# Experts of 448 places with shared half tiles, and row halves for the last channels, in a fused RWKV-7 and hash-routed mixture kernel

## The chip, the cores and the metric

One core of one Trainium2 chip runs the whole kernel. The metric is the device time of one execution in microseconds, as the median of several runs. All arithmetic is in float32.

## The reference

The reference has two stages. The first is a recurrent attention over 768 steps for 4 batches and 8 heads of 40 channels; per head it keeps a 40 x 40 state. Its result is laid out as 3,072 token rows of 320 channels. The second stage sends each row through one of 8 experts, picked by a hash of the token's id.

```python
for t in range(S):                       # S = 768
    y[:, :, t] = einsum('bhd,bhde->bhe', rt, state)
    Sa = einsum('bhde,bhe->bhd', state, at)
    state = state * wt[:, :, None, :] - einsum('bhd,bhe->bhde', Sa, bt) + einsum('bhd,bhe->bhde', vt, kt)
x = y.transpose(0, 2, 1, 3).reshape(3072, 320)
expert_idx = token_ids * 2654435761 % 8
for e in range(8):                       # w1[e]: 320 x 1024, w2[e]: 1024 x 320
    out[mask_e] = maximum(x[mask_e] @ w1[e], 0) @ w2[e]
```

The token ids are drawn with a fixed seed; by them the experts get 387, 359, 415, 376, 364, 403, 371 and 397 tokens.

## The kernel before

**Attention.** The 768 steps are cut into chunks of 64, and two batches make one tile, so there are 24 tiles (`NU`). Each tile passes through a chain of small matrix products (lines 361 to 664), most of them on 40 or 64 rows and 40 or 64 columns of TensorE, with the heads spread over upper and lower row halves and left and right column halves. The order of all this is written out by hand: each piece of work is put into a plan with a tick (`at_tick`, line 249), roughly one tick per tile, and the plan is run sorted by tick (line 800). Engines other than SyncE's queue (SP) keep exactly this order. SP issues the loads of r, v, a, b, k and w (line 240 and others), in program order, each waiting for its buffer. POOL issues the loads of decay products, the stores of finished rows to the DRAM tensor `x_rows` (line 652), and all indirect transfers.

**Routing.** `routing()` (line 688) is a generator whose pieces are put between the attention work from tick 8 on, half a tick apart (line 794). It counts the tokens per expert with two matrix products, gives each token a place in a list of 512 places per expert (`SLOTS`), writes the 3,072 token numbers into the DRAM list `slot_tokens` by 24 indirect writes (line 767), and reads the list back with one transfer (line 774) as `idx_all`, 128 places per column. Empty places hold the number 3,072, and `src_all` is the same list with those cut to the last row.

**Experts.** When attention is done (line 802), the memory of its pools goes to the experts' tiles. Four tiles of 128 places make one expert (`TPE`), and all 512 places are computed. For each expert (line 861):

- `gather` (line 821) brings 128 rows of `x_rows` by an indirect transfer on POOL, turns them with three transposes on TensorE, and has VectorE copy the result into `xt` (lines 831, 832): channels 0 to 127, 128 to 255, and the last 64, by 512 columns.
- `up` (line 834) makes 8 blocks of 128 hidden features. Each block adds three products of 512 columns in one PSUM bank: two over 128 channels and one over the last 64. ScalarE and VectorE take turns at the relu into `ht` (lines 842, 844). A float32 product is two weight loads and two matrix instructions in the trace.
- `down` (line 846) makes, per tile of 128 places, 8 products of 320 columns; ScalarE copies the sum, and POOL scatters the rows to the output (line 853).
- The weights of expert e + 2 are loaded on SP behind expert e (`load_w1`, line 103, with two transfers; `load_w2`, line 816, with one). The weights of experts 0 and 1 are requested on SP as soon as attention's memory is free.

**End.** Lines 874 to 885 sum up whether a decay was out of bounds, and how many overflow tiles there are. Two loops follow, whose counts are read into registers on every engine (lines 899, 944, 945): one recomputes attention in the plain way, the other (line 946) runs overflow tiles one at a time with their weights loaded anew. With these inputs both counts are zero.

Of the kernel before, what the change touches and what calls it, by code (L numbers as in the profile page):

```python
# [40 lines left out]
def kernel(  # L42
# [13 lines left out]
    nc = tc.nc  # L56
# [14 lines left out]
    SLOTS = 512  # L71
    TPE = SLOTS // P
    NST = E * TPE
    NOV = (N - SLOTS) // P
    NT = NST + NOV
    STEP = 8
# [8 lines left out]
    slot_dram = nc.dram_tensor("slot_tokens", (NT * P,), I32)  # L85
# [17 lines left out]
    def load_w1(e, name):  # L103
        t = wpool.tile([P, 3, F], F32, tag="w1", name=name)
        nc.sync.dma_start(t[:, 0:2, :], e[0:2 * P].rearrange("(c p) f -> p c f", p=P))
        nc.sync.dma_start(t[0:DM - 2 * P, 2, :], e[2 * P:DM])
        return t
# [158 lines left out]
    def decays(ri, t0, span, t_f, span_f):  # L266
# [13 lines left out]
        @at_tick(t0 - 1.0)  # L280
        def _():
            x["qb"] = qb = work.tile([P, (HC + 1) * D], F32, tag="qb", name="qb", bufs=1)
            for y in range(2 * RN):
                src = w.rearrange("b h (n t) e -> (b h) n (t e)", t=HC)[:, ri * 2 * RN + y]
                nc.sync.dma_start(qb[y * BH:(y + 1) * BH, 0:HC * D], src)

        @todo.append
        def _():
            x["pb"] = pb = work.tile([P, HC * D], F32, tag="pb", name="pb", bufs=1)

            for i, (sign, at) in enumerate(((-1.0, LO), (1.0, HI))):
                nc.scalar.activation(pb[:], x["qb"][:, 0:HC * D], AF.Relu, bias=lim[:, i:i + 1], scale=sign,
                                     accum_out=wbad[:, 2 * ri + i:2 * ri + i + 1])
# [42 lines left out]
        def _():  # L336
# [3 lines left out]
            store(0, x["pb"][:])  # L340
# [28 lines left out]
    def tile_a(u):  # L369
# [46 lines left out]
        def _():  # L416
# [15 lines left out]
            if ti == 0:  # L432
                groups[gi]["pk"] = work.tile([P, GRP, 2, HP, BLK], F32, tag="pk", name="pk", bufs=1)
# [16 lines left out]
    def group_i(gi, t0, t1, t2):  # L450
# [6 lines left out]
        @at_tick(t0 - 0.5, order=9)  # L457
        def _():
            x["u"] = ub = work.tile([P, BLK, BLK], F32, tag="ub", name="ub", bufs=1)
            nc.gpsimd.memset(ub[:], 0.0)  # L460
            nc.gpsimd.memset(ub[:].rearrange("p s t -> p (s t)")[:, ::BLK + 1], 1.0)

        @at_tick(t0, order=9)
        def _():
            x["n"] = nb = work.tile([P, BLK, BLK], F32, tag="nb", name="nb", bufs=1)
            pk = x["pk"][:].rearrange("p g two h t -> p t (g two h)")
            nc.vector.transpose(nb[:].rearrange("p s t -> p t s"), pk)
# [14 lines left out]
        def _():  # L482
# [4 lines left out]
            nc.vector.transpose(ut[:].rearrange("p g s -> p s g"), ub[:])  # L487
            nc.vector.transpose(ug[:].rearrange("p g t -> p t g"), ub[:].rearrange("p s t -> p t s"))
# [194 lines left out]
    idx_all = route.tile([P, NST], I32)  # L683
    src_all = route.tile([P, NST], I32)
# [3 lines left out]
    def routing():  # L688
# [49 lines left out]
        nc.vector.tensor_scalar(ovt_i[:], ovt[:], float(P - 1), None, op0=OP.add)  # L738
        nc.vector.tensor_scalar(ovt_i[:], ovt_i[:], P.bit_length() - 1, None, op0=OP.logical_shift_right)
# [13 lines left out]
        nc.vector.tensor_scalar(ovtok[:], ovtok[:], float(P), float((NST - TPE) * P), op0=OP.mult, op1=OP.add)  # L753
# [8 lines left out]
        none_t = route.tile([P, NT], I32)  # L762
        nc.vector.memset(none_t[:], N)
        nc.sync.dma_start(slot_dram[:].rearrange("(p c) -> p c", p=P), none_t[:])
        yield
        for c in range(TPP):
# [3 lines left out]
                in_=token[:, c:c + 1], in_offset=None, bounds_check=NT * P - 1, oob_is_err=False)  # L770
# [3 lines left out]
        nc.sync.dma_start(idx_all[:], slot_dram[0:NST * P].rearrange("(c p) -> p c", p=P))  # L774
        yield
# [8 lines left out]
        nc.vector.tensor_scalar(num_i[:], num_i[:], TPE.bit_length() - 1, None, op0=OP.logical_shift_right)  # L784
        nc.vector.tensor_copy(owner[:], num_i[:])
        past = route.tile([1, NOV, E], F32)
        nc.vector.tensor_tensor(past[:], num[:, 0:NOV].unsqueeze(2).to_broadcast([1, NOV, E]),
                                ovin[0:1, :].unsqueeze(1).to_broadcast([1, NOV, E]), op=OP.is_ge)
        nc.vector.tensor_reduce(owner[:, NST:], past[:], axis=AX.X, op=OP.add)
# [4 lines left out]
    for i in range(12 + TPP):  # L794
        at_tick(8 + 0.5 * i, order=7)(lambda: next(steps, None))

    ET = mybir.EngineType
    w1s = {}
# [5 lines left out]
    w1s[0] = load_w1(moe_w1[0], "w1_0")  # L804
# [5 lines left out]
    w1s[1] = load_w1(moe_w1[1], "w1_1")  # L810


    w2pool = pool("w2pool", 2)
    mwork = pool("mwork", 2)

    def load_w2(e, name):
        t = w2pool.tile([P, FP, DM], F32, tag="w2", name=name)
        nc.sync.dma_start(t[:], e.rearrange("(c p) d -> p c d", p=P))
        return t

    def gather(xt, j, idx):

        xg = mwork.tile([P, DM], F32, tag="xg", bufs=6, name="xg")
        nc.gpsimd.indirect_dma_start(out=xg[:], out_offset=None, in_=x_rows[:],  # L824
                                     in_offset=bass.IndirectOffsetOnAxis(ap=idx, axis=0))
        p = bank([P, 3, P], "xg_ps")
        for c in range(3):
            n = min(P, DM - c * P)
            nc.tensor.transpose(p[0:n, c, :], xg[:, c * P:c * P + n], ident[:])  # L829
        q = slice(j * P, (j + 1) * P)  # L830
        nc.vector.tensor_copy(xt[:, 0:2, q], p[:, 0:2, :])  # L831
        nc.vector.tensor_copy(xt[0:DM - 2 * P, 2, q], p[0:DM - 2 * P, 2, :])

    def up(xt, w1, ht, n):
        for f in range(FP):
            p = bank([P, n], "up_ps")
            for c in range(3):
                m = min(P, DM - c * P)
                nc.tensor.matmul(p[:], lhsT=w1[0:m, c, f * P:(f + 1) * P], rhs=xt[0:m, c, 0:n],  # L839
                                 start=(c == 0), stop=(c == 2))  # L840
            if f % 2:
                nc.vector.tensor_scalar(ht[:, f, 0:n], p[:], 0.0, None, op0=OP.max)  # L842
            else:
                nc.scalar.activation(ht[:, f, 0:n], p[:], AF.Relu)  # L844

    def down(ht, w2, j, idx, apart):
        p = bank([P, DM], "dn_ps")
        for f in range(FP):
            nc.tensor.matmul(p[:], lhsT=ht[:, f, j * P:(j + 1) * P], rhs=w2[:, f, :],  # L849
                             start=(f == 0), stop=(f == FP - 1))  # L850
        o = mwork.tile([P, DM], F32, tag="o", bufs=4, name="o")
        nc.scalar.copy(o[:], p[:])  # L852
        st = nc.gpsimd.indirect_dma_start(  # L853
            out=out[:], out_offset=bass.IndirectOffsetOnAxis(ap=idx, axis=0),
            in_=o[:], in_offset=None, bounds_check=N - 1, oob_is_err=False)
# [4 lines left out]
    w2s = {e: load_w2(moe_w2[e], f"w2_{e}") for e in range(2)}  # L860
    for e in range(E):
        xt = mwork.tile([P, 3, SLOTS], F32, tag="xt", name="xt")
        ht = mwork.tile([P, FP, SLOTS], F32, tag="ht", name="ht")
        for j in range(TPE):
            gather(xt, j, src_all[:, e * TPE + j:e * TPE + j + 1])
        up(xt, w1s[e], ht, SLOTS)
        for j in range(TPE):
            down(ht, w2s[e], j, idx_all[:, e * TPE + j:e * TPE + j + 1], True)
        if e + 2 < E:
# [125 lines left out]
```

## Time and profile before

| what | value |
|---|---|
| median of 3 runs | 904.71 us (899.75, 904.71, 911.4) |
| the profiled execution | 892.55 us |
| its span, first to last instruction | 890.8 us |
| TensorE matmul busy | 713.1 us (80%) |
| VectorE, ScalarE, GpSimd busy | 363.8, 284.0, 226.5 us |
| up products (line 839) | 191.9 us |
| down products (line 849) | 140.0 us |
| moved by DMA | 83.06 MB |

The table of the page is over the whole span, while the kernel has two stages with different limits: attention ends at about 510 us, and the experts fill the rest. In the rows below, PE is TensorE's matrix instructions, PEld its weight loads, DVE VectorE, ACT ScalarE, POOL GpSimd and SP SyncE. A granted clock of 1.00 is the 2.4 GHz level and 0.50 the 1.2 GHz level.

### The profile page before, as it was taken

Reading aid. Unit: us, or ns where it says so; the run is one execution under the profiler, and the core shown is the slowest. Engines: PE = TensorE matmul, PEld = TensorE weight load, DVE = VectorE, ACT = ScalarE, POOL = GpSimd, SP = SyncE. Lnnn points to the kernel's source line nnn. Section 1 sums busy time; section 2 is a strip of 40 time slices with the busy share of each in tenths; the row PEclk is TensorE's granted clock in tenths of the full one; section 3 lists DMA queues with packets and bytes.
Section 4 is the critical chain, followed back from the end, with each engine's and each line's share of the span. In section 5 each row is a group of like instructions: output and inputs, shape, how many; then the busy total and the mean of one; then the engine's idle time right before and its main releaser. Section 6 shows DMA issues by size and latency. Waiting matters only on the chain.

```text
span 890.8 us, 25982 instructions
## 1 busy us (share of the span) xinstructions
PE 713.1 (80%) x11284; PEld 488.2 (55%) x11284; DVE 363.8 (41%) x888; ACT 284.0 (32%) x634; POOL 226.5 (25%) x376
## 2 busy tenths in 40 slices
PE   0044558887788887998889839999999999999994
PEld 0033447776677776877778713636353535454543
DVE  7154999789557863665851211110101011110100
ACT  2124246565455654656555301011010101000000
POOL 2113132234243433534222140303030303020101
PEclk9995566798677977879988759999999999999998
DMA  5769676746866965634422190414141414130000
GB/s 95 149 118 182 114 143 125 146 100 113 134 83 105 150 99 95 95 60 52 64 56 55 30 312 1 143 31 150 25 153 34 143 43 127 57 99 1 21 1 24
DMA packets 204195, 83.06 MB, mean 93 GB/s; under 512 B 186926, under 2 KB 195119, under 8 KB 204080
## 3 DMA queue, kind: packets, MB, share of 16 engines
q1 hardware_dynamic: 193328, 52.52, 29.7%
q0 software_dynamic: 10752, 28.87, 14.2%
q8 instruction: 89, 1.46, 0.7%
q14 instruction: 26, 0.21, 0.1%
HBM read 65.58 MB, written 17.08 MB: 93 GB/s over the span
## 4 chain that ended last, share of the span: by engine, by line
PE 69%; DVE 12%; issue 9%; DMA 3%; ACT 3%; SPq 2%; POOL 1%; DVEq 0%; POOLq 0%; ACTq 0%
PE up_ps L839 22%; PE dn_ps L849 16%; PE y_ps L221 5%; PE s_ps L221 4%; PE r_ps L221 3%; PE rc_ps L221 3%; PE t_ps L445 3%; PE a_ps L221 2%; PE u_ps L221 2%; PE z_ps L411 2%; PE x_ps L221 2%; PE sd_ps L660 2%; DVE ub L479 1%; PE c_ps L221 1%; DVE outer L476 1%
## 5 line engine op out<-in xcount | busy, mean ns | idle before, releaser
L839 PE MATMUL up_ps<-xt,w 128*128 128x512 f32 (+1 forms) x384 | 191.9, 630 | 8.6 <-issue 8.1
L849 PE MATMUL dn_ps<-w,ht 128*128 128x320 f32 x512 | 140.0, 434 | 0.0
L839 PEld LDWEIGHTS up_ps<-xt,w 128*128 128x128 f32 (+1 forms) x384 | 62.7, 189 | 133.6 <-issue 132.6
L849 PEld LDWEIGHTS dn_ps<-w,ht 128*128 128x128 f32 x512 | 96.6, 190 | 45.3 <-issue 6.1
L853 POOL DMA_INDIRECT out_dram<-o,idx_all x32 | 31.6, 988 | 272.3 <-ACT o L852 267.1
L842 DVE TENSOR_SCALAR ht<-up_ps 128x512 f32<-128x512 f32 x32 | 22.1, 691 | 174.9 <-PE up_ps L839 139.0
L844 ACT ACTIVATE ht<-up_ps 128x512 f32<-128x512 f32 x32 | 19.1, 597 | 195.0 <-PE up_ps L839 195.0
L479 DVE TENSOR_TENSOR ub<-ub,outer 128x31 f32<-128x31 f32 (+15 forms) x186 | 63.8, 343 | 6.4
L831 DVE COPY xt<-xg_ps 128x256 f32<-128x256 f32 x32 | 13.2, 412 | 128.6 <-PE xg_ps L829 128.6
L476 DVE TENSOR_TENSOR outer<-ub,nb 128x31 f32<-128x31 f32 (+15 forms) x186 | 62.6, 337 | 3.1
L852 ACT COPY o<-dn_ps 128x320 f32<-128x320 f32 x32 | 13.6, 425 | 148.5 <-PE dn_ps L849 148.5
L652 POOL DMA_DIRECT2D x_rows<-xs x48 | 25.4, 536 | 127.9 <-DVE xs L648 67.2
L221 PE MATMUL a_ps<-at_t,z_t 40*64 40x64 f32 x1536 | 38.4, 251 | 21.1 <-ACT z_t L413 15.3
L531 POOL MEMSET x<- 64x512 f32 x48 | 25.0, 520 | 104.6 <-PE s_ps L221 101.5
L221 PEld LDWEIGHTS a_ps<-at_t,z_t 40*64 40x64 f32 x1536 | 32.9, 159 | 29.1 <-ACT z_t L413 20.1
L323 PE MATMUL f_ps<-own,partner 128*128 128x40 f32 x12 | 3.6, 401 | 54.9 <-DVE own L318 53.3
L383 POOL DMA_DIRECT2D pl<-p_rows x48 | 25.7, 535 | 78.3 <-DVE at L396 51.7
L411 PE MATMUL z_ps<-ident,z 128*104 128x128 f32 x192 | 39.5, 376 | 1.3 <-DVE z L398 1.3
L824 POOL DMA_INDIRECT xg<-x_rows,src_all x32 | 31.0, 967 | 34.0 <-PE xg_ps L829 19.0
L648 DVE TENSOR_TENSOR xs<-y_ps,py 128x320 f32<-128x320 f32 x24 | 11.8, 490 | 63.0 <-PE y_ps L221 62.0
L615 DVE TENSOR_TENSOR mr<-rc_ps,after 128x1024 f32<-128x1024 f32 x24 | 29.3, 1222 | 18.3 <-PE rc_ps L221 18.3
L445 PE MATMUL t_ps<-ident,at 128*104 128x128 f32 x96 | 23.6, 393 | 15.6 <-DVE at L396 15.1
(159 smaller groups left out, 1171.3 us busy)
## 6 DMA issues: line engine op xcount, KB each, us to landing
w<-in_moe_w_dram SPq DMA_DIRECT2D x8, 1280.0 KB
w<-in_moe_w_dram SPq DMA_DIRECT2D x8, 1024.0 KB
ql<-q_rows POOLq DMA_DIRECT2D x48, 160.0 KB
qb<-in_w_dram SPq DMA_DIRECT2D x24, 160.0 KB
al<-in_a_dram SPq DMA_DIRECT2D x48, 80.0 KB
kb<-in_b_dram SPq DMA_DIRECT2D x48, 80.0 KB
kb<-in_k_dram SPq DMA_DIRECT2D x48, 80.0 KB
r<-in_r_dram SPq DMA_DIRECT2D x48, 80.0 KB
```

The lines of the kernel that those rows point to most:

```text
L221: nc.tensor.matmul(out_, lhsT=lhsT, rhs=rhs, start=start, stop=stop, skip_group_check=True)
L383: nc.gpsimd.dma_start(pl[half(be)], of_batches(p_rows, 2 * g + be, 1))
L411: nc.tensor.transpose(p[0:R, be, hp * P:(hp + 1) * P], x["z"][:, be, hp, :], ident[:])
L445: nc.tensor.transpose(p[0:R, hp, :], src[:, hp, 0:R], ident[:])
L476: nc.vector.tensor_tensor(tv, ub[:, 0:j + 1, j:j + 1].to_broadcast([P, j + 1, m]), nb[:, j, j + 1:].unsqueeze(1).to_broadcast([P, j + 1, m ...
L479: nc.vector.tensor_tensor(o, o, tv, op=OP.add)
L615: nc.vector.tensor_tensor(t[:].rearrange("p two h t -> p (two h) t"), p[:].rearrange("p two (h t) -> p (two h) t", t=C), after[:].unsqueez ...
L652: nc.gpsimd.dma_start(x_rows[r0:r0 + C, :], xs[half(be), :])
L824: nc.gpsimd.indirect_dma_start(out=xg[:], out_offset=None, in_=x_rows[:], in_offset=bass.IndirectOffsetOnAxis(ap=idx, axis=0))
L839: nc.tensor.matmul(p[:], lhsT=w1[0:m, c, f * P:(f + 1) * P], rhs=xt[0:m, c, 0:n], start=(c == 0), stop=(c == 2))
L849: nc.tensor.matmul(p[:], lhsT=ht[:, f, j * P:(j + 1) * P], rhs=w2[:, f, :], start=(f == 0), stop=(f == FP - 1))
L853: st = nc.gpsimd.indirect_dma_start(out=out[:], out_offset=bass.IndirectOffsetOnAxis(ap=idx, axis=0), in_=o[:], in_offset=None, bounds_che ...
```

## The change

**Places.** An expert has 448 places instead of 512: three tiles of 128 (`TPE = 3`) and one half tile of 64. The half tiles of two neighbours (experts 0 and 1, 2 and 3, ...) lie in one index column, so that one gather and one scatter serve both. The list in DRAM is read back with ten transfers instead of one. Overflow tiles have 64 places. The routing starts at tick 7 instead of 8, and its end is cut into more pieces.

**Up.** The last 64 channels of w1 are stored twice as compactly: blocks of even number on partitions 0 to 63, blocks of odd number on 64 to 127, side by side. The last 64 channels of the turned rows are therefore copied to both halves of the partitions. Blocks are computed four at a time: first all eight products over 128 channels into four banks, then the four products over 64 channels, which alternate between upper and lower rows, then the four relus.

**Down.** The three full tiles are as before. The two half tiles of a pair are computed after the odd expert: for each block of features one product of 64 weight columns with the even expert's w2 into PSUM partitions 0 to 63, and one with the odd expert's into 64 to 127.

**Order.** The gathers of the next expert are issued before `up` of this one, and its transposes and copies are put between `up` and `down` of this one. The experts' order is written by hand on all engines but SP. Expert 0's weights are requested on SP at tick 28 (`NU + 4`) into buffers of a pool of their own, which attention has done with by then; those of experts 1 and 2 on POOL, behind the gathers of experts 0 and 1; those of 3 to 7 on SP behind the down products of the second expert before. w2 has three buffers beside the early one. The sums of the check (`rest()`) stand between `up` and `down` of the last expert, and one loop around both loops, passed when neither has work, takes the place of two.

```diff
-    SLOTS = 512
+    SLOTS = 448
     TPE = SLOTS // P
+    SZ = 64
...
+    early = pool("early", 1)
+
+    def load_w1(t, e, dma):
+        for c in range(2):
+            dma(t[c], e[c * P:(c + 1) * P])
+        for i in range(2):
+            dma(t[2][i * SZ:(i + 1) * SZ].rearrange("p (f x) -> p f x", x=P),
+                e[2 * P:DM].rearrange("p (f two x) -> two p f x", two=2, x=P)[i])
+
+    def load_w2(t, e, dma):
+        for i in range(2):
+            dma(t[i], e[i * FH:(i + 1) * FH].rearrange("(c p) d -> p c d", p=P))
+
+    def early_weights():
+        t1 = [early.tile([P, F], F32, tag=n, name=f"w1_0{n}")[:] for n in ("pk", "nb", "ub")]
...
+        load_w1(w1s[0], moe_w1[0], nc.sync.dma_start)
+        load_w2(w2s[0], moe_w2[0], nc.sync.dma_start)
...
-    for i in range(12 + TPP):
-        at_tick(8 + 0.5 * i, order=7)(lambda: next(steps, None))
+    for i in range(24 + TPP):
+        at_tick(7 + 0.5 * i, order=7)(lambda: next(steps, None))
+
+    at_tick(NU + 4.0)(early_weights)
...
+    def place(xt, c0, p, cols):
+        to = slice(c0, c0 + cols.stop - cols.start)
+        nc.vector.tensor_copy(xt[:, 0:2, to], p[:, 0:2, cols])
+        for i in range(2):
+            nc.vector.tensor_copy(xt[i * SZ:(i + 1) * SZ, 2, to], p[0:SZ, 2, cols])
+
+    UPS = 4
 
     def up(xt, w1, ht, n):
+        for f0 in range(0, FP, UPS):
+            ps_ = [bank([P, n], "up_ps") for _ in range(UPS)]
+            for i, p in enumerate(ps_):
+                for c in range(2):
+                    nc.tensor.matmul(p[:], lhsT=w1[c][:, (f0 + i) * P:(f0 + i + 1) * P], rhs=xt[:, c, 0:n],
+                                     start=(c == 0), stop=False)
+            for i, p in enumerate(ps_):
+                rows = slice(i % 2 * SZ, (i % 2 + 1) * SZ)
+                q = (f0 + i) // 2 * P
+                nc.tensor.matmul(p[:], lhsT=w1[2][rows, q:q + P], rhs=xt[rows, 2, 0:n], start=False, stop=True)
...
+    def down(parts, idx, apart):
+        p = bank([P, DM], "dn_ps")
+        m = P // len(parts) if apart else SZ
         for f in range(FP):
...
+            for i, (ht, w2, c0) in enumerate(parts):
+                nc.tensor.matmul(p[i * m:(i + 1) * m], lhsT=ht[:, f, c0:c0 + m], rhs=w2[f // (FP // 2)][:, f % (FP // 2), :],
+                                 start=(f == 0), stop=(f == FP - 1), skip_group_check=True)
...
+    def rows_of(e):
+        tiles_ = [tile_of(e, j) for j in range(TPE)] + [shared_tile(e)] * (e % 2 == 0)
+        return [gather(src_all[:, t]) for t in tiles_]
...
+    with tc.manual_schedule(engines={ET.PE, ET.DVE, ET.Activation, ET.Pool}):
+        xt = columns_of(0, rows_of(0))
+        weights(1, moe_w1[1], moe_w2[1], nc.gpsimd.dma_start)
+        for e in range(E):
+            xgs = rows_of(e + 1) if e + 1 < E else None
+            if e == 0:
+                weights(2, moe_w1[2], moe_w2[2], nc.gpsimd.dma_start)
+            ht = mwork.tile([P, FP, SLOTS], F32, tag="ht", name="ht")
+            up(xt, w1s[e], ht, SLOTS)
+            if xgs is None:
+                rest()
+            else:
+                xt = columns_of(e + 1, xgs)
+            for j in range(TPE):
+                down([(ht, w2s[e], j * P)], idx_all[:, tile_of(e, j)], True)
+            mine = (ht, w2s[e], TPE * P)
+            if e % 2:
+                down([partner_, mine], idx_all[:, shared_tile(e)], True)
+            partner_ = mine
+            if 0 < e < E - 2:
+                weights(e + 2, moe_w1[e + 2], moe_w2[e + 2], nc.sync.dma_start)
...
+    some = nc.values_load(ctl_i[0:1, 3:4], min_val=0, max_val=1)
+    with tc.For_i(0, some, 1):
```

## Rows read from the trace of the kernel before

**Rows 1.** Windows, two stages: us, each engine's busy us, granted clock, DMA share, GB/s

```profile
300.00:450.00 150.00, 129.68 (x3940) 111.81 (x3942) 95.61 (x231) 85.52 (x193) 56.98 (x96) 0.84 0.52 80
...
560.00:600.00 40.00, 38.84 (x112) 18.64 (x111) 4.40 (x12) 4.09 (x8) 7.87 (x8) 1.00 0.23 73
```

**Rows 2.** Chain of waits in order of time: one expert, and the end

```profile
576.07 23.77 PE up_ps L839 x48
599.84 17.42 PE dn_ps L849 x64
617.26 1.31 PE xg_ps L829 x12
618.57 1.16 issue
...
879.27 0.13 PE bad_ps L877 x2
```

**Rows 3.** Timeline, first up products of an expert: start us, us, engine, line

```profile
575.56 0.41 DVE L831 COPY xt<-xg_ps 128x256 f32<-128x256 f32 x1
...
576.57 0.19 PEld L839 LDWEIGHTS up_ps<-xt,w 128*128 128x128 f32 x1 [0.24 <-issue]
...
577.00 0.19 PEld L839 LDWEIGHTS up_ps<-xt,w 128*128 128x128 f32 x1 [0.24 <-issue]
577.95 0.29 PEld L839 LDWEIGHTS up_ps<-xt,w 64*128 64x128 f32 x2 [0.76 <-issue]
...
579.00 0.30 PEld L839 LDWEIGHTS up_ps<-xt,w 128*128 128x128 f32 x2 [0.76 <-issue]
```

**Rows 4.** Timeline in attention at the full clock: products on column halves and quadrants

```profile
490.94 0.78 PE L221 MATMUL r_ps<-x,mk 128*64 128x80 f32 x16
...
491.64 0.43 PE L553 MATMUL v_ps<-ident,x 64*104 64x64 f32 x8
...
492.34 0.66 PE L221 MATMUL c_ps<-um,r 64*40 64x64 f32 x32 [0.26 <-ACT r L579]
```

**Rows 5.** Timeline from the last attention rows to the first up products

```profile
511.03 1.05 POOL L652 DMA_DIRECT2D x_rows<-xs  x2 [4.16 <-DVE xs L648]
...
519.46 1.02 POOL L824 DMA_INDIRECT xg<-x_rows,src_all  x1 [7.37 <-DMA w<-in_moe_w_dram]
...
525.46 0.45 PEld L829 LDWEIGHTS xg_ps<-ident,xg 128*128 128x128 f32 x3 [15.41 <-issue]
...
530.65 25.52 PE L839 MATMUL up_ps<-xt,w 128*128 128x512 f32 x48 [0.52 <-DVE xt L831]
```

**Rows 6.** Windows, the wait before the first up products

```profile
520.00:530.60 10.60, 3.58 (x12) 1.79 (x12) 2.28 (x8) 0.00 (x0) 8.07 (x9) 0.50 1.05 352
```

**Rows 7.** One line's instructions: slot writes, duration min/median/max in ns, first and last start

```profile
L767 POOL DMA_INDIRECT slot_tokens<-token,key_i x24: 1025/1037/1252, 215.4 to 421.2; - x24
```

**Rows 8.** Timeline of SP's queue late in attention

```profile
424.44 0.41 SPq L774 DMA_DIRECT2D idx_all<-slot_tokens  x1
...
466.12 1.28 SPq L240 DMA_DIRECT2D x<-in_v_dram  x2
...
479.69 1.28 SPq L240 DMA_DIRECT2D x<-in_v_dram  x2
```

**Rows 9.** Groups by line on POOL: busy us, mean ns of one | idle before

```profile
L824 POOL DMA_INDIRECT xg<-x_rows,src_all x32 | 31.0, 967 | 34.0 <-PE xg_ps L829 19.0 <-DMA w<-in_moe_w_dram 7.4 <-issue 4.3
...
L384 POOL DMA_DIRECT2D ql<-q_rows x48 | 25.4, 529 | 8.7 <-DVE z L398 4.1 <-DMA q_rows<-qb 3.6 <-DVE qb L309 0.3
```

**Rows 10.** Chain of waits late in attention: a stall

```profile
461.57 2.17 issue
```

**Rows 11.** Windows of TensorE alone after that stall

```profile
463.70:474.90 11.20, 11.16 (x225) 0.50 0.11 18
```

**Rows 12.** One line's instructions: second loop's register load and last branch, ns and starts

```profile
L944 ACTq TENSOR_LOAD <-ctl_i x1: 278/278/278, 883.1 to 883.1; - x1
...
L946 POOLq COMPARE_BRANCH x3: 33/33/39, 884.0 to 886.3; - x3
```

More of the change, by code (lines that the diff above doesn't have):

```diff
@@ L281, in _ @@
         def _():
-            x["qb"] = qb = work.tile([P, (HC + 1) * D], F32, tag="qb", name="qb", bufs=1)
+            x["qb"] = qb = early.tile([P, (HC + 1) * D], F32, tag="qb", name="qb")
             for y in range(2 * RN):
@@ L808, in bank, with weights, gather, turned @@
         return ps.tile(shape, F32, tag="ps", name=name)
-    w1s[1] = load_w1(moe_w1[1], "w1_1")
-    w2pool = pool("w2pool", 2)
     mwork = pool("mwork", 2)
[L816 to L824, printed above, removed]
+    def weights(e, w1, w2, dma):
+        t = wpool.tile([P, 2 * F + FH], F32, tag="w1", name=f"w1_{e}")
+        w1s[e] = [t[:, 0:F], t[:, F:2 * F], t[:, 2 * F:]]
+        t = wpool.tile([P, FP, DM], F32, tag="w2", name=f"w2_{e}", bufs=3)
+        w2s[e] = [t[:, 0:FP // 2], t[:, FP // 2:]]
+        load_w1(w1s[e], w1, dma)
+        load_w2(w2s[e], w2, dma)
+    def gather(idx, m=P):
+        xg = mwork.tile([P, DM], F32, tag="xg", bufs=8, name="xg")
+        nc.gpsimd.indirect_dma_start(out=xg[0:m], out_offset=None, in_=x_rows[:],
                                      in_offset=bass.IndirectOffsetOnAxis(ap=idx, axis=0))
+        return xg[0:m]
+    def turned(xg):
+        m = xg.shape[0]
         p = bank([P, 3, P], "xg_ps")
@@ L846, in down @@
[L846 to L850, printed above, removed]
+            nc.tensor.transpose(p[0:n, c, 0:m], xg[:, c * P:c * P + n], ident[0:m, 0:m])
+        return p
+    def place(xt, c0, p, cols):
+        to = slice(c0, c0 + cols.stop - cols.start)
+        nc.vector.tensor_copy(xt[:, 0:2, to], p[:, 0:2, cols])
+        for i in range(2):
+            nc.vector.tensor_copy(xt[i * SZ:(i + 1) * SZ, 2, to], p[0:SZ, 2, cols])
@@ L858, in down @@
             tc.add_to_no_dep_group("out_rows", st.ins)
-    w2s = {e: load_w2(moe_w2[e], f"w2_{e}") for e in range(2)}
-    for e in range(E):
-        xt = mwork.tile([P, 3, SLOTS], F32, tag="xt", name="xt")
[L863 to L869, printed above, removed]
-            w1s[e + 2] = load_w1(moe_w1[e + 2], f"w1_{e + 2}")
-            w2s[e + 2] = load_w2(moe_w2[e + 2], f"w2_{e + 2}")
@@ new lines, in tile_of, with shared_tile, columns_of @@
+    def tile_of(e, j):
+        return slice(e * TPE + j, e * TPE + j + 1)
+    def shared_tile(e):
+        return tile_of(E, e // 2)
+    def rows_of(e):
+        tiles_ = [tile_of(e, j) for j in range(TPE)] + [shared_tile(e)] * (e % 2 == 0)
+        return [gather(src_all[:, t]) for t in tiles_]
+    def columns_of(e, xgs):
+        xt = mwork.tile([P, 3, SLOTS], F32, tag="xt", name="xt")
+        for j, xg in enumerate(xgs):
+            p = turned(xg)
+            if j < TPE:
+                place(xt, j * P, p, slice(0, P))
+            else:
+                place(xt, TPE * P, p, slice(0, SZ))
+                others[0] = mwork.tile([P, 3, SZ], F32, tag="other", name="other")
+                place(others[0], 0, p, slice(SZ, P))
+        if e % 2:
+            nc.vector.tensor_copy(xt[:, :, TPE * P:], others[0][:])
+        return xt
```

270 lines of the change are left out of this document (141 added, 129 removed).

## The prediction

> **What bounds the kernel now.** I read the stages first, in the table of windows. In the attention stage TensorE is busy 86% of the time at a mean clock of 0.84, and VectorE and ScalarE are busy 57 to 64%; in the expert stage TensorE is busy 97% at the full clock of 2.4 GHz, and every other engine is under 20% [rows 1]. So in the expert stage only TensorE's own work, and what it waits for at a seam, can change the time. The chain of waits says how that work is made up: every expert is 23.77 us of up products, 17.42 us of down products, 1.31 us of transposes and 1.16 us in which TensorE does nothing; expert 0's up products begin at 530.65, and the last down product ends at 879.27 [rows 2, 5]. That is 348.6 us of 890.8.
>
> Then I took the up products apart in the order of time. Two weight loads in a row stand 0.43 us apart, which is one product of 512 columns; but the load for the 64-row piece comes with its product's start, not under the one before, and so does the next load for 128 rows: they stand 1.05 us apart, where two products take 0.865 [rows 3]. So each change between 128 and 64 rows costs 0.188 us. Check: 6 x 0.4325 + 2 x 0.188 = 2.971, an eighth of 23.77. Down products take 17.42/64 = 0.272 us for 320 columns. Both kinds therefore cost 0.85 ns per column, and 448 columns will cost about 0.379 us.
>
> **The change, part by part.**
>
> *Up.* A block of 128 features now needs four instructions over all rows and two over half the rows, at 448 columns. Full rows: 8 x 4 x 0.379 = 12.13 us per expert. Half rows: 16 x 0.379 = 6.06 us in line; 3.03 if upper and lower rows run side by side. Nearest rows for halves that alternate: 16 products of 80 columns into column halves stood 0.70 us ahead of the next group, where 16 x 80 x 0.85 ns is 1.09; 32 products on quadrants of 64 columns took 0.66 instead of 1.74 [rows 4]. So halves do overlap: 1.6 times at least (short products, ends included), 2.6 times with four quadrants. At 448 columns I take 2 times, plus half a product of stagger at the end of each group of four blocks (0.19 x 2): 3.41 us. Bounds: 3.03 and 6.06. Changes of shape: one in and one out per group of four blocks, 4 x 0.188 = 0.75 instead of 16. Sum 16.29 against 23.77; over eight experts **-59.8 us**.
>
> *Down.* 24 full tiles remain, at 4.355 each (104.5). The eight halves make four shared tiles of 32 instructions into column halves: 4.36 us at twice the rate, 0.14 stagger, 0.38 for two changes of shape: 4 x 4.88 = 19.5. Sum 124.0 against 139.4: **-15.4 us**. Bounds: four shared tiles at 4.36, and at 8.71 in line.
>
> *Transposes and the gap.* 24 tiles instead of 28 between experts, 0.328 us each: 7.9 us. The gap of 1.16 us was VectorE's copies of the turned rows (the last began at 575.56, the products at 576.07) [rows 3]. They now run beside the down products before, which last 13 us; VectorE had 4.4 busy us in 40 [rows 1], so the split copies of the 64-channel piece are hidden. Seven seams of 2.47 us become 7.9 us: **-9.4 us**. If that cover failed, the gap would only be back. Next in line would be the gathers, issued at the start of the up products 16 us earlier; four of them take about 5 us of POOL and 5 to land [rows 5].
>
> *Start of the experts.* The last attention rows are issued by 512.08, but the first gather starts at 519.46 and its rows arrive at 525.46, 5.0 us after its issue [rows 5], while weights move at 352 GB/s [rows 6]. Away from such traffic, the load that needed the last slot write was issued at 424.44, 2.2 us after that write's issue ended (421.2 + 1.04) [rows 7, 8]. In the changed kernel the weights of expert 0 are moved ahead, and those of experts 1 and 2 behind the first gathers on POOL. So: rows landed 514.3, four gathers of 1.27 until 519.4, landed 521.6, three transposes and a copy (1.4): 523.0 instead of 530.65, **-7.6 us**. Bounds: 0 and -8. The moved weights cost POOL twelve issues. A request of 64 rows took 0.53 us, one of 128 rows 0.97 [rows 9]; the pieces of w2 have 512 separate rows and those of w1's last channels 256, so I bound them between 0.53 each and 7.6 ns per row: 3 to 14 us per expert. Behind them stand expert 1's gathers: issued by 537 at worst, landed by 542, wanted at about 541. I take nothing, and 4 us at worst. The first scatter comes later.
>
> *Attention.* Routing starts one step earlier and is a dozen small VectorE instructions and nine SP requests longer; at 0.41 us a request [rows 8] that is 4 us of SP's queue, with the r and v loads behind it, less than the slack that v has below. Expert 0's weights (2.6 MB, some 7.4 us at 352 GB/s) go on SP's queue after about 467, ahead of the last tile's r and v loads. Its v was issued at 479.69 and is wanted at 491.64 [rows 4, 8]; so they should pass. The price of a stall here is larger than the stall: after one of 2.17 us at 461.57 [rows 10] the granted clock stood at 0.50, the 1.2 GHz level, for the next 11 us [rows 11], some 5 us of lost work. I take **+2 us**; bounds -5 (that stall goes) and +14 (two new ones).
>
> *End.* The check now runs under the last down products, and one empty loop is passed instead of two: from the second loop's register loads at 883.1 to its last branch at 886.3 [rows 12], **-3.2 us**; bounds 0 and -4.
>
> The sum is -93.4 us. The profiled execution took 892.55 us, span 890.8: 799.1. That execution stands 12.2 us under the median of the three runs shown, 904.71, which itself lies between 899.75 and 911.4. I see no reason for the excess to shrink, so the forecast for a median is 811 us.
>
> **A rule against it.** The rows show loads for 128 rows starting 0.43 us apart under running products of the same rows, and no load visible in the down products [rows 2, 3]. The Trainium skill, "TensorE: Matmul & The Clock Gate", Part 3, says that a weight load overlaps running products only where the row group differs. By that rule the column halves, which all use 128 rows, would pay every load (a rival below); the rows here disagree, so I do not charge it. The same part measures packing of long products at 2.38 times for three column tiles and 3.07 for four row tiles, about 0.78 of the ideal; an estimate from this page is 1.55 times for two, and a time of about 820.
>
> **Rivals.**
>
> *Halves run in line or nearly so* (0.11). For: all overlap seen is in products of 40 to 80 columns, none at 320 or 448. Against: rows 4. In line, up gains 8 x 2.65 less and down 4 x 4.21 less: +38 us, 849. At the 1.6 times of the row, 0.4 more per expert in up and 0.9 per shared tile in down: 818, inside the forecast.
>
> *Column halves pay for their weight loads* (0.03). If no load into a column half could start while the other half runs on the same rows, the 128 loads of the shared tiles would each show their 0.19 us: +24 us, 835. Against: the load of 0.19 us at 577.00 is hidden under a product of the same rows [rows 3].
>
> *The moved weights disturb the last attention tiles* (0.12). SP or the engines' requests wait behind 2.6 MB, and TensorE loses its clock as it did after 461.57. Two or three stalls at 7 us each: 825 to 832. For: that row. Against: r and v have 12 us of slack.
>
> *The clock* (0.03). If the halves' pattern left the expert stage at the 1.2 GHz level, TensorE's 262 us there would grow by 2.6 us per per cent of the stage. From 36% of it the gain is gone, and from 43% it is slower than the 2%; throughout, some 1,070 us. For: tiled products in attention are seen at 0.50 [rows 11]. Against: there a stall came first, and the expert stage, at the full clock with a gap of 1.16 us per expert, gets shorter gaps.
>
> *Experts that run over* (0.01). With more than 448 tokens an expert's rest goes through the loop at the end, one 64-place tile at a time, weights loaded anew: at least 7.4 us for weights, 5 for a gather and some 6 of products. The reference's own token list, with its fixed seed, puts 359 to 415 tokens on an expert, so no iteration runs.
>
> **Numbers.** The forecast (0.70) covers 795 to 825. The range is 788 to 846: below, a median without half of the 12 us excess and with the best bounds of start and attention; above, the disturbed tiles and halves that overlap hardly. About what a measurement here can tell from no change is 2%, or 18 us; only the clock and mishaps in attention several times those priced reach it. Faster 0.95, within 2% 0.03, slower 0.02.
>
> **What would show it.** In the changed profile: per expert about 16.3 us of up products and 13.1 of down, 17.9 with the shared tile; no idle before the next up; full-row loads 0.38 us apart; eight half-row instructions in about 1.7 us (3.0 if in line); first up at about 523; one loop at the end. The forecast is wrong if shared tiles take 8.7 us, if the clock is under 1.00 in the expert stage, if transposes for expert 1 wait for their gather, or if the last xs comes later than 510.

## The result, and the profile after

The changed kernel takes 807.24 us as the median of four runs, the kernel before 902.25 us as the median of its four (the three shown and one more beside the changed kernel). The ratio of 0.890, with a 95% interval of 0.879 to 0.901, and the ratios further below are of means that leave out executions in a slower state of the chip (here 812.46 us, one of the changed kernel's four). The profiled execution took 798.80 us (span 797.0), 93.75 us less than the one before.

The windows of the same two stages [rows 1] (us, busy us of PE, PEld, DVE, ACT and POOL, granted clock, DMA share, GB/s) show where it went:

```profile
300.00:450.00 150.00, 128.61 (x3858) 110.34 (x3850) 91.48 (x214) 82.97 (x187) 51.86 (x86) 0.82 0.53 90
560.00:600.00 40.00, 40.00 (x156) 22.54 (x155) 6.36 (x19) 4.31 (x9) 11.33 (x12) 1.00 0.31 98
```

Attention is nearly as it was. In the expert stage TensorE is now busy all the time at the same full clock. The chain of waits, from the down products of expert 0 through all of expert 1 to the first up products of expert 2 [rows 2]:

```profile
546.26 1.13 PE xg_ps L874 x9
547.39 12.92 PE dn_ps L909 x48
560.31 6.01 PE up_ps L891 x16
566.33 1.71 PE up_ps L896 x8
568.03 6.21 PE up_ps L891 x16
574.24 1.71 PE up_ps L896 x8
575.95 1.46 PE xg_ps L874 x12
577.40 17.38 PE dn_ps L909 x80
594.78 6.21 PE up_ps L891 x16
```

Line 891 holds the up products over 128 channels, line 896 those over the last 64. Up is 15.6 to 15.8 us instead of 23.77 (17.8 for expert 0, whose first products run at the 1.2 GHz level), and no gap is left between down and up. Eight instructions on half rows take 1.71 us. The shared tile takes 17.38 - 12.92 = 4.46 us, for 32 instructions of 320 columns that would take 8.6 in line. In the timeline of that tile, the two halves' instructions start at most 0.01 us apart:

```profile
591.38 0.43 PE L909 MATMUL dn_ps<-w_0qb,ht 128*64 128x320 f32 x1
591.39 0.43 PE L909 MATMUL dn_ps<-w,ht 128*64 128x320 f32 x1
```

The start is the part that came out otherwise. The timeline, SP and POOL, from the last attention rows on [rows 5]:

```profile
510.21 0.94 SPq L121 DMA_DIRECT2D w<-in_moe_w_dram  x2
510.90 1.04 POOL L679 DMA_DIRECT2D x_rows<-xs  x2 [4.16 <-DVE xs L675]
...
518.11 1.02 POOL L865 DMA_INDIRECT xg<-x_rows,src_all  x1 [6.17 <-issue]
...
521.96 0.94 POOL L865 DMA_INDIRECT xg<-x_rows,src_all  x1 [0.30 <-issue]
522.90 1.20 POOL L114 DMA_DIRECT2D w<-in_moe_w_dram  x2
...
527.14 0.45 PEld L874 LDWEIGHTS xg_ps<-ident,xg 128*128 128x128 f32 x3 [3.03 <-DMA xg<-x_rows,src_all]
...
528.43 1.86 PE L891 MATMUL up_ps<-xt,w_0pk 128*128 128x448 f32 x2 [0.38 <-DVE xt L880]
```

At 510.21, just ahead of the last attention rows, SP requests a whole w2 that the prediction did not count on. It is not expert 0's, which SP requested long before:

```profile
352.47 0.61 SPq L121 DMA_DIRECT2D w_0qb<-in_moe_w_dram  x1
353.13 0.50 SPq L121 DMA_DIRECT2D w_0pb<-in_moe_w_dram  x1
```

SP's order is not written by hand, so tick 28 does not bind it either: the halves of expert 0's w2 went at 352 and 353, and the pieces of its w1 between 419 and 460, where the prediction had all of them after 467. And w2 has three buffers: expert 3's w2 needs nothing but free memory, and memory comes free at the end of attention. The first gather starts 8.0 us behind the last attention rows (VectorE's product, 510.12) instead of 9.2, and the first up products 18.3 us behind instead of 20.4.

Against the profiled execution before, in us:

| part | forecast | measured |
|---|---|---|
| attention, to the last rows' product | +2 | -0.1 (510.25 to 510.12) |
| start, from there to the first up | -7.6 | -2.1 (20.40 to 18.31) |
| up | -59.8 | -64.0 (191.9 to 127.9) |
| down | -15.4 | -18.2 (139.4 to 121.2) |
| transposes, gaps between the stages | -9.4 | -7.1 |
| end | -3.2 | -2.3 (11.4 to 9.1 from the last copy) |
| sum | -93.4 | -93.8 |

Each measured term is the sum of TensorE's pieces of that kind, from the chain and, where the chain runs through POOL (from 695 us on), from the timeline; the gaps hold a new wait of 1.3 us ahead of the last down products, where TensorE waits for the sum of the check.

### The profile page after: what moved, and what is told of

Read it like the earlier page. It is cut to its first block, busy times and chain, and to the rows that moved or that the text cites. A ratio compares the mean times of both kernels' runs of the same rounds, so it can differ in the third digit from the quotient of the medians.

```text
span 797.0 us, 25924 instructions
## 1 busy us (share of the span) xinstructions
PE 630.0 (79%) x11272; PEld 466.4 (59%) x11272; DVE 373.5 (47%) x925; ACT 281.7 (35%) x630; POOL 227.7 (29%) x381
## 3 DMA queue, kind: packets, MB, share of 16 engines
q0 software_dynamic: 11712, 33.46, 18.2%
## 4 chain that ended last, share of the span: by engine, by line
PE 55%; issue 17%; DVE 13%; ACT 5%; DMA 4%; SPq 3%; POOL 2%; POOLq 0%; DVEq 0%; ACTq 0%
PE dn_ps L909 9%; PE up_ps L891 9%; PE y_ps L247 5%; PE s_ps L247 4%; PE r_ps L247 4%; PE rc_ps L247 3%; PE t_ps L472 3%; PE a_ps L247 2%; PE u_ps L247 2%; PE z_ps L437 2%; PE up_ps L896 2%; PE sd_ps L687 2%; PE x_ps L247 2%; DVE outer L503 2%; DVE ub L506 2%
## 5 line engine op out<-in xcount | busy, mean ns | idle before, releaser
L899 DVE TENSOR_SCALAR ht<-up_ps 128x448 f32<-128x448 f32 x32 | 20.0, 625 | 196.1 <-PE up_ps L896 130.2
L909 PE MATMUL dn_ps<-w,ht 128*128 128x320 f32 (+1 forms) x448 | 109.5, 433 | 0.0
L909 PEld LDWEIGHTS dn_ps<-w,ht 128*128 128x128 f32 (+1 forms) x448 | 72.0, 177 | 32.1 <-issue 1.3
L891 PE MATMUL up_ps<-xt,w 128*128 128x448 f32 x224 | 87.5, 544 | 0.0
L914 POOL DMA_INDIRECT out_dram<-o,idx_all x28 | 27.6, 987 | 197.9 <-ACT o L913 179.8
L891 PEld LDWEIGHTS up_ps<-xt,w 128*128 128x128 f32 x224 | 41.7, 190 | 43.1 <-issue 37.9
L901 ACT ACTIVATE ht<-up_ps 128x448 f32<-128x448 f32 x32 | 17.4, 545 | 136.1 <-PE up_ps L896 101.7
L247 PE MATMUL a_ps<-at_t,z_t 40*64 40x64 f32 x1536 | 37.6, 250 | 20.4 <-ACT z_t L439 13.2
L463 ACT COPY pk<-a_ps 128x256 f32<-128x256 f32 x24 | 8.9, 373 | 82.6 <-DVE mk L455 78.9
L437 PEld LDWEIGHTS z_ps<-ident,z 128*104 128x104 f32 x192 | 34.5, 186 | 2.4 <-issue 1.2
L349 PEld LDWEIGHTS f_ps<-own,partner 128*128 128x128 f32 x12 | 2.9, 290 | 54.6 <-DVE own L344 53.9
```

The lines of the kernel that those rows point to most:

```text
L247: nc.tensor.matmul(out_, lhsT=lhsT, rhs=rhs, start=start, stop=stop, skip_group_check=True)
L437: nc.tensor.transpose(p[0:R, be, hp * P:(hp + 1) * P], x["z"][:, be, hp, :], ident[:])
L891: nc.tensor.matmul(p[:], lhsT=w1[c][:, (f0 + i) * P:(f0 + i + 1) * P], rhs=xt[:, c, 0:n], start=(c == 0), stop=False)
L899: nc.vector.tensor_scalar(ht[:, f0 + i, 0:n], p[:], 0.0, None, op0=OP.max)
L909: nc.tensor.matmul(p[i * m:(i + 1) * m], lhsT=ht[:, f, c0:c0 + m], rhs=w2[f // (FP // 2)][:, f % (FP // 2), :], start=(f == 0), stop=(f == ...
L914: st = nc.gpsimd.indirect_dma_start(out=out[:], out_offset=bass.IndirectOffsetOnAxis(ap=idx, axis=0), in_=o[0:m], in_offset=None, bounds_c ...
```

## The experiments

Every kernel is the changed one with one edit, or with several where that is said. All share its attention code (one leaves out the early request of weights), and yet the last rows' product came anywhere from 504.4 to 523.7 us in their executions. So they are compared from there on: 18.31 us to the first up products, and from those 268.57 us to the end, in the changed kernel. Each of these times is of one execution. Where an edit leaves a stretch alone, other executions took 18.3 to 19.2 us and 267.9 to 269.2, so a difference under 1 us says nothing.

**Order of the row halves.**

```diff
-            for i, p in enumerate(ps_):
+            for i, p in [(i, ps_[i]) for i in (0, 2, 1, 3)]:
                 rows = slice(i % 2 * SZ, (i % 2 + 1) * SZ)
```

> The changed kernel with one edit: the four products over the last 64 channels in a group run in the order lower, lower, upper, upper rows instead of alternating. Theory (alternating halves run side by side, which is worth 3 us per expert): with at most one product of overlap left in the middle, eight half-row instructions take 7 or 8 times 0.376 us plus one change of shape, 2.8 to 3.2 us, instead of 1.71 us; with 16 groups the kernel is 18 to 24 us longer. Rival (each half has a queue of its own, so that order does not matter): still 1.7 us and no change of the time. Rival (no overlap in either): 3.2 us would already stand in the changed kernel, which its trace denies.

Measured: 268.28 us, no change, and the chain still reads

```profile
564.14 1.71 PE up_ps L896 x8
```

The order did change: in the timeline the relu of the second block, which VectorE starts 0.04 us behind ScalarE's first in the changed kernel (567.35 and 567.31), now comes 0.8 us behind it: it waits for a count of finished blocks, and the second block is now third in the order.

```profile
565.12 0.55 ACT L901 ACTIVATE ht<-up_ps 128x448 f32<-128x448 f32 x1 [6.53 <-PE up_ps L896]
...
565.91 0.62 DVE L899 TENSOR_SCALAR ht<-up_ps 128x448 f32<-128x448 f32 x1 [17.57 <-PE up_ps L896]
```

So my theory of strict order fell: the upper rows' products ran beside the lower ones that stand before them.

**All on the lower rows.**

```diff
-                rows = slice(i % 2 * SZ, (i % 2 + 1) * SZ)
+                rows = slice(0, SZ)
```

> The changed kernel with all products over the last 64 channels on the lower rows, so that blocks of odd number take the even block's last channels of w1. Theory (what halves the time of these products is that they lie on different rows): eight such instructions take 8 x 0.376 + 0.19 = 3.2 us instead of 1.71, and the kernel is 16 x 1.5 = 24 us longer. Rival (a product over 64 rows is by itself twice as fast at this length): 1.7 us, no change; this would also explain why the order lower, lower, upper, upper cost nothing.

Measured: 292.21 us, 23.6 more, and in the chain

```profile
567.72 3.20 PE up_ps L896 x8
```

This is the theory's number. It is lying on different rows that halves the time, not the order and not the length.

**Order of the column halves.**

```diff
-        for f in range(FP):
-            for i, (ht, w2, c0) in enumerate(parts):
+        for i, (ht, w2, c0) in enumerate(parts):
+            for f in range(FP):
```

> The changed kernel with one edit: in a shared tile all products of the even expert's half come first, then all of the odd one's, instead of alternating between the column halves. Theory (column halves run side by side only where neighbours in the order lie on different halves): a shared tile takes 32 x 0.269 = 8.6 us plus the changes of shape instead of 4.46; four tiles make the kernel about 17 us longer. Rival (the gain lies in the 64 columns, not in running side by side): 4.5 us and no change.

Measured: 281.21 us, 12.6 more, and a shared tile of 20.66 - 12.92 = 7.74 us: most of what strict order would cost, but not all.

```profile
578.88 20.66 PE dn_ps L909 x80
```

The timeline of TensorE in the first shared tile shows why. Expert 0's half reads `w_0qb` and `w_0pb`, expert 1's half reads `w`, and all of the former stand first in the program:

```profile
591.74 2.37 PE L909 MATMUL dn_ps<-w_0qb,ht 128*64 128x320 f32 x8
593.94 1.51 PE L909 MATMUL dn_ps<-w_0pb,ht 128*64 128x320 f32 x5
595.02 0.48 PE L909 MATMUL dn_ps<-w,ht 128*64 128x320 f32 x1
595.29 0.43 PE L909 MATMUL dn_ps<-w_0pb,ht 128*64 128x320 f32 x1
595.34 0.43 PE L909 MATMUL dn_ps<-w,ht 128*64 128x320 f32 x1
595.56 0.43 PE L909 MATMUL dn_ps<-w_0pb,ht 128*64 128x320 f32 x1
595.61 0.43 PE L909 MATMUL dn_ps<-w,ht 128*64 128x320 f32 x1
595.83 0.43 PE L909 MATMUL dn_ps<-w_0pb,ht 128*64 128x320 f32 x1
```

The first product of expert 1's half starts at 595.02, before three instructions that precede it in the program (595.29, 595.56 and 595.83). Four steps of 0.269 us run double: 28 steps and a change of shape are 7.7 us.

**Runs of four.**

```diff
-        for f in range(FP):
-            for i, (ht, w2, c0) in enumerate(parts):
+        for i, f in [(i, f) for f0 in (0, 4) for i in range(len(parts)) for f in range(f0, f0 + 4)]:
+            for ht, w2, c0 in parts[i:i + 1]:
```

> The changed kernel with the shared tile's products in runs of four per half (eight instructions) instead of alternating one by one. Theory, formed after the two runs on order (a product may start ahead of up to about four instructions that come before it, if it lies on the other half): each change of half overlaps four instructions and no more, so 20 steps of 0.269 us and a change of shape, 5.6 us per shared tile instead of 4.46, and 4.5 us over four tiles. Rival (strict order, a product starts only when all before it have started): 29 steps, 8.0 us. Rival (each half has a long queue of its own): 4.5 us, which the run with sixteen in a row denies unless the queue is about that long.

Measured: 273.33 us, 4.8 more; the shared tile is 18.62 - 12.92 = 5.70 us.

```profile
590.81 18.62 PE dn_ps L909 x80
```

That agrees with a reach of about four matrix instructions and with neither rival. The timeline of this run's first shared tile has it at each of the three changes of half: the next run's first instruction starts beside the last but three of the run before (604.79, 605.93 and 607.06).

**Groups of two blocks.**

```diff
-    UPS = 4
+    UPS = 2
```

> The changed kernel with up products in groups of two blocks instead of four: the same products, but four changes to half rows and four back per expert instead of two and two. Theory (each change of shape costs 0.188 us): 0.75 us more per expert, 6 us over eight; four half-row instructions take 0.75 + 0.19 us. Rival (the changes cost nothing beside running products): no difference. Rival (relus of two banks now hold up the next group): more than 10 us, with gaps on TensorE.

Measured: 274.99 us, 6.4 more, and no gap:

```profile
577.84 0.95 PE up_ps L896 x4
578.79 3.20 PE up_ps L891 x8
```

The theory said 6. The price of a change of shape that the prediction took from the kernel before holds.

**The seam as before.** The transposes and copies of the next expert go behind the down products.

```diff
             if xgs is None:
                 rest()
-            else:
-                xt = columns_of(e + 1, xgs)
...
             partner_ = mine
+            if xgs is not None:
+                xt = columns_of(e + 1, xgs)
```

> The changed kernel with the transposes and copies of the next expert put back behind the down products; its gathers stay early. Theory (the gap before the up products was VectorE's copies, and the down products cover it in the changed kernel): TensorE stands still for 1.2 us or a little more before each of seven up stages, since a tile is now three copies instead of two, and one copy more for the shared half; 8 to 12 us longer from the first up products to the end. Rival (copies are fast enough, the gap was something else): no gap.

Measured: 295.97 us, 27.4 more where the theory said 8 to 12, or 3.9 per seam on average. The gap is there, 2.58 us long ahead of the experts of odd number and 2.24 ahead of the others, and the copies are its cause; but it costs more than its length. Windows of the gap and of the products soon after it, in the first seam:

```profile
569.74:572.30 2.56, 0.00 (x0) 0.00 (x0) 2.43 (x8) 0.00 (x0) 1.95 (x3) 1.00 0.17 64
573.50:576.70 3.20, 3.20 (x5) 1.33 (x4) 0.00 (x0) 0.00 (x0) 1.74 (x2) 0.51 0.48 126
```

TensorE stands still while VectorE is busy with the copies, and the granted clock is soon after at the 1.2 GHz level for about 3.2 us. This did not follow every gap. The first group of up products shows it, in the second seam without such a tail and in the third with one:

```profile
611.18 6.25 PE L891 MATMUL up_ps<-xt,w 128*128 128x448 f32 x16 [2.24 <-issue]
...
643.74 7.97 PE L891 MATMUL up_ps<-xt,w 128*128 128x448 f32 x16 [2.58 <-DVE xt L961]
```

It took 7.86 to 7.98 us in five of the seven seams, behind all four gaps of 2.58 us and one of 2.24, and 6.25 behind the other two gaps of 2.24. Seven gaps (17.0 us) and five tails of 1.7 us make 25.5 of the 27.4. The gap of 1.16 us before [rows 2] had no tail. What decides between the gaps of 2.24 us stays open.

**Two buffers for w2.**

```diff
-        t = wpool.tile([P, FP, DM], F32, tag="w2", name=f"w2_{e}", bufs=3)
+        t = wpool.tile([P, FP, DM], F32, tag="w2", name=f"w2_{e}", bufs=2)
```

> The changed kernel with two buffers instead of three for w2, so that expert 3's w2 cannot be requested when attention's memory comes free, at 510, but only after expert 1's down products. Theory (that request's 1.28 MB hold up the last attention rows on their way to DRAM, which land at 516.6 instead of about 513.5): no weights move between 510 and the first gather, the first gather starts at about 515 instead of 518.1 from the same end of attention, and the first up products 2 to 3 us earlier, near 525.5 where attention ends at 510.1; expert 3's w2 comes about 595 and is waited for by nobody. Rival (the rows' way takes 5 us in any case, with the semaphore waits behind it): the first gather stays 8 us behind the last attention rows.

Measured: 15.15 us to the first up products instead of 18.31, then 269.2. The first gather starts 4.9 us behind the last rows' product (518.65) instead of 8.0:

```profile
519.43 1.05 POOL L679 DMA_DIRECT2D x_rows<-xs  x2 [4.15 <-DVE xs L675]
523.58 1.02 POOL L865 DMA_INDIRECT xg<-x_rows,src_all  x1 [3.10 <-issue]
```

The chain's wait for the last rows on their way to DRAM, in this run:

```profile
519.95 2.06 DMA x_rows<-xs
```

And in the changed kernel:

```profile
511.42 5.13 DMA x_rows<-xs
```

The theory holds: without the 1.28 MB the rows are waited for 3.1 us less.

**And expert 1's weights behind expert 1's gathers.**

```diff
         xt = columns_of(0, rows_of(0))
-        weights(1, moe_w1[1], moe_w2[1], nc.gpsimd.dma_start)
         for e in range(E):
             xgs = rows_of(e + 1) if e + 1 < E else None
             if e == 0:
+                weights(1, moe_w1[1], moe_w2[1], nc.gpsimd.dma_start)
```

> As the kernel with two buffers for w2, and expert 1's weights are issued on POOL behind expert 1's gathers instead of before them. Theory (in the changed kernel the fourth gather of expert 0 lands 4.2 us after its issue because expert 1's weights move at 350 GB/s by then): it lands 2.2 to 2.5 us after its issue, the first up products start 2 us earlier than with two buffers alone, and 4 to 5 us earlier than in the changed kernel, 13.5 to 14 us behind the last attention rows' issue instead of 17.5; up products of expert 1 wait for nothing. Rival (gathers land late by themselves, after some 4 us): no difference to two buffers alone.

Measured: 14.21 us, then 267.91. The chain's wait for the fourth gather, from its issue, is 3.83 us, after 5.13 in the changed kernel and 5.04 with two buffers alone. In this run:

```profile
529.18 3.83 DMA xg<-x_rows,src_all
```

And in the changed kernel:

```profile
521.96 5.13 DMA xg<-x_rows,src_all
```

About 0.9 us of the issue is in it, so the landing took 2.9 us instead of 4.2: the direction of the theory, and two thirds of its size. The first up products come 0.9 us earlier than with two buffers alone, not 2, and that alone is no more than the spread; the wait itself is outside it, since every run that issues expert 1's weights first waited 5.0 to 5.8 us.

**Expert 0's weights not early.**

```diff
-    at_tick(NU + 4.0)(early_weights)
...
+        weights(0, moe_w1[0], moe_w2[0], nc.sync.dma_start)
         xt = columns_of(0, rows_of(0))
```

> The changed kernel with expert 0's weights requested on SP when attention's memory comes free, as before, instead of during attention. Theory (weights that move while the last attention rows and the first gathers are on their way hold these up): the rows land 6 us or more behind the last request, and the first up products start 20 us or more behind the last attention rows instead of 18.3. Rival (weights do not get in the way, or not more than expert 3's w2 already does): 18.3 us. In the stage before, no effect beyond the spread of that stage in all runs.

Measured: 18.62 us, then 267.97. The theory fell: the early request alone brings nothing beyond the spread of 18.3 to 19.2 us. Here expert 0's weights take the third w2 buffer, so expert 3's are not requested: 2.6 MB at this point cost the start about as much as 1.28 MB do. The timeline shows that only the first 1.0 MB (line 114) is requested ahead of the last attention rows:

```profile
504.53 0.83 SPq L114 DMA_DIRECT2D w<-in_moe_w_dram  x2
505.19 1.05 POOL L679 DMA_DIRECT2D x_rows<-xs  x2 [4.16 <-DVE xs L675]
505.71 1.27 SPq L116 DMA_DIRECT2D w<-in_moe_w_dram  x2
507.03 1.19 SPq L121 DMA_DIRECT2D w<-in_moe_w_dram  x2
```

That may be why the amount matters so little; no run tries it.

**Two loops at the end.**

```diff
-    with tc.For_i(0, some, 1):
+    if True:
```

> The changed kernel without the loop around the two loops at its end: both counts are read and both empty loops are passed one after the other, as before; the check's sums stay ahead of the last down products. Theory (each empty loop is a turn of all engines of its own): the end, from the last down product to the last instruction, is 11 to 12 us instead of 9.2, as in the kernel before. Rival (the last scatter's way to DRAM and the final drain set the end): 9.2 us still.

Measured: 268.78 us from the first up products, 0.2 more; from the last copy to the last instruction 9.4 us instead of 9.1, where the other executions took 8.5 to 9.3. The theory fell. Most of the 2.3 us that the end gained did not come from the loop; what came of moving the check's sums ahead was not tried by itself.

**The edits of the start together, and the check ahead of the last up products.** Three edits: the two above, and a third that puts the call of `rest()` before `up` of the last expert.

> Both edits at the start (two buffers for w2, expert 1's weights behind expert 1's gathers), and the check's sums ahead of the last up products instead of behind them, so that TensorE does not wait 0.9 us for VectorE's sum before the last down products. Theory: from the last attention rows to the first up products 14.2 us instead of 18.3; from there to the end 267 us instead of 268.6; 5 to 6 us, 0.7%, faster than the changed kernel by medians over several rounds. Rival (the spread of the attention stage, some 16 us over the runs so far, hides it): the medians cannot be told apart.

Measured: 13.80 us to the first up products, then 268.13. The wait ahead of the last down products is gone, yet the rest is only 0.4 us shorter than in the changed kernel; a slower first group of up products (8.60 us instead of 8.21) takes back 0.4 us. The median of six is 798.39 us, the ratio to the kernel before (median 894.39 us on this chip) 0.891, 0.885 to 0.897.

**The changed kernel beside it.**

> The changed kernel itself once more, on the same chip as the version with the two edits at the start, to compare their medians: 804 to 810 us, and 18.3 us from the last attention rows to the first up products.

Measured: 799.84 us as the median of six, below the 804 to 810 expected, on a chip where the kernel before is faster too; ratio 0.895, 0.889 to 0.901; 18.42 us to the first up products, then 268.25. The traces differ by 4.6 us at the start; the medians differ by 1.45 and the intervals overlap, so they don't show that the other version is faster.

## Why the prediction was right

It was right in sign, in size and in the greater part of its steps. That the sum came within 0.4 us of the profiled execution is luck: up, down and attention came out 9.1 us better than forecast, and start, gaps and end 8.7 us worse.

*Up and down.* The price per column from the kernel before held at 448 columns (0.376 us per instruction against 0.379), as did the price of a change of shape. The halves ran side by side in full. The stagger that I added, 0.38 us per expert for up and 0.14 per shared tile, is not there: the halves start at most 0.01 us apart. It makes 3.6 of the 7.0 us by which up and down came out shorter than forecast.

*Transposes.* The gap went, under the cover that the prediction named. The sentence "If that cover failed, the gap would only be back" was wrong: without the cover a seam costs not 1.16 us but 3.9 on average, since the copies are longer now and the clock fell behind five of the seven gaps.

*Start.* The step that failed is "In the changed kernel the weights of expert 0 are moved ahead": it priced the start as if no weights moved there, 12.8 us from the last rows' product to the first up products, and 18.3 were measured. With three buffers one more expert's w2 fits, and SP asks for it at the worst moment. The run with two buffers takes this away and saves 3.2 us; it puts the first gather where the theory without traffic has it within a microsecond (3.1 us behind the end of the request instead of 2.2; nine waits on semaphores and a pause, 1.6 us together, stand between). The second miss is expert 1's weights, which move while the fourth gather lands: behind expert 1's gathers, they let it land in 2.9 us instead of 4.2, where the forecast had 2.2. With both edits the start takes 13.8 and 14.2 us in two traces; in the shorter it is 6.6 us shorter than before, against the forecast 7.6. The early request of expert 0's weights, to which the prediction gave the gain, brings nothing that shows as the kernel stands.

*Attention and the median.* Nothing disturbed the last tiles: from the twenty-first tile's rows to the last, all fourteen traces took 25.3 to 26.5 us, also those without an early request. From the fifteenth to the twenty-first, while the pieces of w1 are requested, the spread is wide (69.1 to 83.3 us), and the two without the request lie within it (72.2 and 75.3). The sign "if the last xs comes later than 510" tells nothing: it was set at the kernel before's own 510.25, the profiled execution had 510.12, and others of the same code came up to 523.7. The 12 us between the profiled execution and a median was not a constant: it was 8.4 us after. What differs between the traced executions is when attention ends; from its last rows on, the changed kernel took 286.9 and 286.7 us in two of them. Why attention's end varies stays open. The lower end of the range, 788, does not follow from the terms named for it: half of the excess, -8 for the start and -5 for attention give about 798.

*Rivals.* Halves in line, column halves that pay for their loads, and a fall of the clock in the expert stage did not happen: the shared tile took 4.46 us, and the granted clock is 1.00 from 540 to 767 us. The rule of the Trainium skill, "TensorE: Matmul & The Clock Gate", Part 3, by which a load overlaps products only on other row groups, would have made a shared tile longer by its 32 loads. A load of 64 columns takes 0.14 us in the trace (the prediction charged the 0.19 of 128 columns), so that is 4.4 us more; the tile measured 4.46 us, 16 steps of 0.269 and 0.16 over, and denies it. The packing rates of the same Part of the Trainium skill, 2.38 for three and 3.07 for four tiles, from which the prediction estimated 1.55 for two, were exceeded here: 8 instructions on two row halves took 1.71 us against 3.20 on one, which is 1.9 times, and 2.0 without the change of shape.

## What to carry to other kernels

Price a product by its columns from a row of the same kernel, and price the change of array shape by itself, since grouping products by shape can be worth nearly as much as making them shorter: here 12 changes fewer per expert are 2.3 us, and 48 instructions shorter by 0.056 us are 2.7. When a change gives a buffer pool one more buffer, ask which transfer it lets loose, and when: a transfer that waits for nothing goes at the first moment that memory is free, ahead of the small ones on which the next stage hangs. And take executions apart at the stage that the edit touches, where the spread of another stage hides it.

## What was not expected of the hardware

- A matrix instruction can start ahead of three that stand before it in the program, beside the fourth, if it lies on other rows or columns of the array. Runs of four instructions per row half cost nothing; on column halves, runs of eight cost 1.2 us per shared tile and runs of sixteen 3.3 us.
- Two halves run at twice the rate of one at 320 and at 448 columns, and start at most 0.01 us apart when they alternate.
- Of seven gaps on TensorE in a stage at the 2.4 GHz level, all four of 2.58 us and one of three of 2.24 us were followed by a stretch at the 1.2 GHz level that cost 1.6 to 1.7 us; the other two of 2.24 us and the gaps of 1.16 us in the kernel before were not.
- With a weight transfer of 1.28 MB requested just before, the chain waits 5.13 us for the last 80 KB of rows on their way to DRAM instead of 2.06; 2.6 MB, of which 1.0 MB was requested ahead of the rows, held up the start of the gathers no longer (7.7 us behind the last rows' product, 8.0 with 1.28 MB).
